# Two result rows in one PSUM bank, copied out by halves of their columns

## The chip, the cores and the metric

The kernel runs on one core of a Trainium2 chip. The metric is the device time of one execution in microseconds. The kernel before took 80.83 us (median of 3 runs, 80.6 to 80.95).

## The reference

One token `x` of 512 numbers goes through two branches whose results are mixed by a gate. Only the last 4096 positions of the caches of 65,536 are used.

```python
def _A_ref(x, k_cache, v_cache, wq, wo):      # 32 heads of queries, 8 of keys and values, 128 each
    W = min(4096, max(256, Sk // 4))          # 4096
    q = (x @ wq) as (heads, 1, 128)
    k, v = the last W positions of the caches, each repeated for 4 query heads
    p = _softmax((q · k) * 128 ** -0.5)
    return (p · v as 4096 numbers) @ wo       # 512

def _B_ref(x, w_gate, w_up, w_down):          # 512 -> 1792 -> 512
    return (_sigmoid(x @ w_gate) * (x @ w_up)) @ w_down

g = _sigmoid((x * gate_w).sum(-1, keepdims=True))
return g * _A_ref(...) + (1 - g) * _B_ref(...)
```

All inputs and the output are bf16. The output is one row of 512.

## The kernel before, in words

About 30 MB are read: `wq`, four pairs of K heads (`kn`), the gate and up weights, `wo`, four pairs of V heads (`vv`) and `w_down`, nearly all on the sync engine's DMA queue in the order of their use. The order of TensorE, VectorE and ScalarE is that of the text (`manual_schedule`, L187); only semaphore waits stand between them, and the framework puts those in from the tiles that an instruction reads and writes.

The queries are made first (L210 to L226), then the scores: each half pair of K is transposed by VectorE (L198) and multiplied into the score banks `S_ps` (L237). Softmax is by a maximum (L253 to L268), an exponential on ScalarE (L275) and a transpose to `eT` (L277). The gate and up projections (`glu`, L247) are put between these steps; each writes the partition groups 0, 32, 64 and 96 of one PSUM bank. For each pair of V heads, 16 matmuls (L316) sum into `pv_ps`. `pv_copy` (ScalarE, L322) moves two pairs' sums to SBUF, `heads_out` (L327 to L329) brings them into heads and divides by the softmax sum, and `heads_rows` (L334 to L336) leaves them as columns of `oY`.

The last step is the one that the change touches. `add_row` (L301 to L304) multiplies one column of 128 numbers by 512 columns of `wo` or `w_down`. It does it as two matmuls of 256 columns, one whose result is on partition 0 and one whose result is on partition 32, so that they use different column groups of the TensorE array. Both results accumulate in the PSUM tile `a_ps`, which spans two banks: the left half of the output row is in the first bank, the right half in the second. `out_rows` calls it for 32 columns of `oY` (64 matmuls) and the loop at L359 for 14 columns of `hT` (28 matmuls). In L358 and L359 the last 60 of these 92 follow one another.

Then the two halves are brought out (L362 to L366). VectorE copies row 0, 256 columns, to SBUF, and the sync queue stores it; ScalarE copies row 32, 256 columns, and its own queue stores it. Each store is one piece of 512 B.

Of the kernel before, what the change touches and what calls it, by code (L numbers as in the profile page):

```python
# [12 lines left out]
BF16 = mybir.dt.bfloat16  # L13
F32 = mybir.dt.float32
# [3 lines left out]
def kernel(  # L18
# [14 lines left out]
    nc = tc.nc  # L33

    P = 128
# [12 lines left out]
    N_OUT = A_wo.shape[1]  # L48
# [19 lines left out]
    work = ctx.enter_context(tc.tile_pool(name="work", bufs=1))  # L68
    ps_big = ctx.enter_context(tc.tile_pool(name="ps_big", bufs=2, space=bass.MemoryType.PSUM))
    ps_S = ctx.enter_context(tc.tile_pool(name="ps_S", bufs=2, space=bass.MemoryType.PSUM))  # L70
# [37 lines left out]
    wo_sb = big.tile([P, 2, NC_H, N_OUT], BF16, name="wo_sb", tag="big")  # L108
# [82 lines left out]
    for u in range(4):  # L191
        nc.tensor.matmul(S_ps[u // 2][:, u % 2, :], lhsT=other[:].rearrange("p o y u -> p (o y u)"),  # L192
                         rhs=ident[0:2, 0:2].rearrange("p (o y) -> p o y", o=1).to_broadcast([2, 256, 2]),
# [12 lines left out]
    for k in range(8):  # L206
        q_ps = ps_big.tile([P, 512], F32, name="q_ps", tag="b")
        ks = slice(k * 512, (k + 1) * 512)
        for c in range(DC):
            nc.tensor.matmul(q_ps[:], lhsT=xT[:, c:c + 1].to_broadcast([P, P]),  # L210
                             rhs=wq_sb[:, c, ks], start=(c == 0), stop=(c == DC - 1))
# [18 lines left out]
    for a in range(HP):  # L230
        for v in range(2):
            kT = kTs[a, v] if (a, v) in kTs else k_transpose(a, v)
            k_v = kT[:].rearrange("p (n dhi s t) -> p n dhi s t", n=KB, dhi=2, s=32)
            for dhi in range(2):
                for t in range(2):
                    for hb in range(2):
                        nc.tensor.matmul(S_ps[v][:, hb, :], lhsT=q_st[:, a, dhi, :, t],  # L237
                                         rhs=k_v[:, hb * 16:(hb + 1) * 16, dhi, :, t],
# [57 lines left out]

    HN = N_OUT // 2
    pv_ps = ps_S.tile([P, 2, 4 * P], F32, name="pv_ps", tag="S")
    a_ps = ps_S.tile([P, 2, 512], F32, name="a_ps", tag="S")

    def add_row(lhsT, rhs, start, stop):  # L301
        for i in range(2):
            nc.tensor.matmul(a_ps[32 * i:32 * i + 1, i, 0:HN], lhsT=lhsT, rhs=rhs[:, i * HN:(i + 1) * HN],  # L303
                             start=start, stop=stop)  # L304


# [5 lines left out]
    oY = work.tile([P, 2, NC_H], BF16, name="oY")  # L312
# [24 lines left out]

    def out_rows(hf, c0, c1):
        for c in range(c0, c1):
            add_row(oY[:, hf, c:c + 1], wo_sb[:, hf, c, :], hf == 0 and c == 0, False)  # L340

    pv(0)

# [8 lines left out]
    pv(3)  # L352
    pv_copy(1)
    out_rows(0, 0, NC_H // 2)
    heads_out(1)
    out_rows(0, NC_H // 2, NC_H)
    heads_rows(1)
    out_rows(1, 0, NC_H)  # L358
    for j in range(NJ):  # L359
        add_row(hT[:, j, 0:1], wd_sb[:, j, :], False, j == NJ - 1)  # L360

    res = work.tile([P, HN], BF16, name="res")  # L362
    nc.vector.tensor_copy(res[0:1, :], a_ps[0:1, 0, 0:HN])  # L363
    nc.sync.dma_start(out[0, :, 0:HN], res[0:1, :])
    nc.scalar.copy(res[32:33, :], a_ps[32:33, 1, 0:HN])
    nc.scalar.dma_start(out[0, :, HN:N_OUT], res[32:33, :])  # L366


# [28 lines left out]
```

## Time and profile before

| what | value |
|---|---|
| time, median of 3 | 80.83 us |
| span of the profiled execution | 80.0 us |
| TensorE busy | 56.9 us (71%) |
| VectorE busy | 39.2 us (49%) |
| ScalarE busy | 11.4 us (14%) |
| bytes read | 30.67 MB, 383 GB/s over the span |
| mean granted TensorE clock | 0.936 |
| last matmul issued to `a_ps` | 77.1 us, 272 ns long |

In the profile, L12 is line 12 of the kernel's source; DVE is VectorE, ACT is ScalarE, PE is TensorE, PEld its loads of the stationary operand, SPq and ACTq the sequencers of the sync engine and of ScalarE, which issue DMAs. A row of the timeline has the start, the length, the engine, the line, the operation, what is written and read, the shapes, and in brackets how long the engine had been idle and what released it. The chain of waits is followed back from the last instruction, at each step to what released it.

### The profile page before, as it was taken

To read this page: it belongs to the slowest core of one execution; us is meant where nothing else is said; L and a number is where in the kernel's file an instruction comes from. 1 tells how busy PE (TensorE), PEld (TensorE's weight loads), DVE (VectorE), ACT (ScalarE), POOL (GpSimd) and SP (SyncE) were. 2 spreads that over 40 slices of the span, in tenths; PEclk is the share of its full clock that TensorE was granted. 3 is DMA by queue.
4 is the path that set the end of the run, shared out by engine and by line. 5 is a ranking of instruction groups with operands and counts; after the bars stand their busy time and mean duration, and the time that the engine had idled before them with its cause. 6 is when DMAs were issued, how large, how long until landed. Compare 5 with 4: busy or idle time off the path is not lost.

```text
span 80.0 us, 833 instructions
## 1 busy us (share of the span) xinstructions
PE 56.9 (71%) x329; PEld 25.8 (32%) x329; DVE 39.2 (49%) x51; ACT 11.4 (14%) x21; POOL 3.7 (5%) x13
## 2 busy tenths in 40 slices
PE   0200194999941999988889365999698099998960
PEld 0200131333410334433333122444245033366840
DVE  0600820039449999999995519999500100002020
ACT  2400000225653000000000283000200000020010
POOL 7910000000000000000000000000000000000000
PEclk9999999999999579999999999999999755599999
DMA  6789989999999999999999999999999999998400
GB/s 181 262 344 525 426 360 393 434 451 426 410 459 434 410 451 414 444 392 425 407 449 467 401 401 451 459 393 410 451 430 385 430 459 451 381 393 344 152 0 1
DMA packets 2682, 30.71 MB, mean 384 GB/s; under 512 B 308, under 2 KB 440, under 8 KB 760
## 3 DMA queue, kind: packets, MB, share of 16 engines
q1 hardware_dynamic: 2674, 30.67, 91.3%
q8 instruction: 2, 0.03, 0.2%
q10 hardware_dynamic: 6, 0.00, 0.0%
HBM read 30.67 MB, written 0.00 MB: 383 GB/s over the span
## 4 chain that ended last, share of the span: by engine, by line
DMA 60%; PE 16%; DVE 14%; issue 4%; SPq 2%; DVEq 0%
DMA kn<-in_A_k_cache_dram 31%; DMA vv<-in_A_v_cache_dram 29%; DVE kT L198 13%; PE pv_ps L316 8%; PE a_ps L303 7%; SPq L85 2%; PE o_ps L327 1%; SPq L81 1%; DVE res L363 1%; DVE oY L336 0%; PE oY_ps L334 0%; DVEq L198 0%
## 5 line engine op out<-in xcount | busy, mean ns | idle before, releaser
L316 PE MATMUL pv_ps<-vv,eT 128*32 128x512 bf16 x64 | 17.4, 432 | 4.0 <-DMA vv<-in_A_v_cache_dram 1.7
L237 PE MATMUL S_ps<-kT,qbig 128*128 128x512 bf16 x64 | 16.3, 407 | 3.9 <-DVE qbig L226 2.8
L198 DVE STREAM_TRANSPOSE kT<-kn 128x2048 f32<-128x2048 f32 x8 | 17.8, 2278 | 0.0
L316 PEld LDWEIGHTS <-eT 128*32 128x32 bf16 x64 | 6.7, 107 | 13.7 <-issue 5.8
L237 PEld LDWEIGHTS <-qbig 128*128 128x128 bf16 x64 | 6.5, 102 | 13.7 <-issue 4.5
L210 PE MATMUL q_ps<-wq_sb,xT 128*128 128x512 bf16 x32 | 9.9, 484 | 1.2 <-DMA wq_sb<-in_A_wq_dram 1.2
L328 DVE TENSOR_TENSOR oT<-o_ps,rb 128x16 bf16<-128x16 f32 x2 | 0.3, 175 | 14.6 <-PE o_ps L327 14.6
L215 DVE STREAM_TRANSPOSE qtT<-q_sb 128x512 f32<-128x512 f32 x4 | 2.8, 712 | 8.0 <-ACT q_sb L212 8.0
L210 PEld LDWEIGHTS <-xT 128*128 128x128 bf16 x32 | 3.8, 118 | 7.8 <-issue 5.9
L192 PE MATMUL S_ps<-ident,other 2*128 2x512 bf16 x4 | 2.0, 611 | 5.7 <-DVE other L147 5.7
L212 ACT CAST q_sb<-q_ps 128x512 bf16<-128x512 f32 x8 | 4.7, 585 | 8.2 <-PE q_ps L210 8.2
L303 PE MATMUL a_ps<-wo_sb,oY 128*1 128x256 bf16 x64 | 5.2, 275 | 0.3 <-DVE oY L336 0.3
L322 ACT COPY pv_sb<-pv_ps 64x512 f32<-64x512 f32 x2 | 1.2, 578 | 21.4 <-PE pv_ps L316 21.4
L277 DVE STREAM_TRANSPOSE eT<-e_sb 128x1024 bf16<-128x1024 bf16 x2 | 2.4, 1224 | 1.9 <-ACT e_sb L275 1.9
L258 ACT ACTIVATE sge<-gu_ps 128x448 f32<-128x448 f32 x1 | 0.5, 543 | 18.9 <-PE gu_ps L247 18.9
L303 PEld LDWEIGHTS <-oY 128*1 128x1 bf16 x64 | 2.8, 83 | 1.2 <-DVE oY L336 0.4
L287 DVE RECIPROCAL sg<-sge 128x448 f32<-128x448 f32 x1 | 3.0, 2953 | 0.0
L175 DVE TENSOR_TENSOR gpr<-xr 1x512 f32<-1x512 bf16 x1 | 0.7, 680 | 4.6 <-DMA xr<-in_gate_w_dram 4.6
L253 DVE TENSOR_REDUCE pm<-S_ps 128x1 f32<-128x1024 f32 x2 | 2.4, 1204 | 0.9 <-PE S_ps L237 0.9
L155 PE MATMUL xt_ps<-ident,xr 1*128 1x1 bf16 x4 | 0.3, 164 | 3.5 <-POOL ident L131 3.5
L192 PEld LDWEIGHTS <-other 2*128 2x128 bf16 x4 | 0.6, 158 | 6.0 <-DVE other L147 5.8
L163 DVE COPY xp<-xr 1x64 bf16<-1x64 bf16 x2 | 1.2, 1162 | 2.0 <-DMA xr<-in_A_x_dram 2.0
(65 smaller groups left out, 33.5 us busy)
## 6 DMA issues: line engine op xcount, KB each, us to landing
kn<-in_A_k_cache_dram SPq DMA_DIRECT2D x4, 2048.0 KB, 20.9
vv<-in_A_v_cache_dram SPq DMA_DIRECT2D x3, 2048.0 KB, 19.4
wq_sb<-in_A_wq_dram SPq DMA_DIRECT2D x1, 4096.0 KB
wo_sb<-in_A_wo_dram SPq DMA_DIRECT2D x2, 2048.0 KB
vv<-in_A_v_cache_dram SPq DMA_DIRECT2D x2, 1024.0 KB
wg_sb<-in_B_w_gate_dram SPq DMA_DIRECT2D x1, 1792.0 KB
wu_sb<-in_B_w_up_dram SPq DMA_DIRECT2D x1, 1344.0 KB
wd_sb<-in_B_w_down_dram SPq DMA_DIRECT2D x1, 1024.0 KB
```

What stands on the lines that cost most here:

```text
L85: dq.dma_start(t[:, n0:n1, :].rearrange("p n d -> p (n d)"), cache[0, 2 * a:2 * a + 2, SBASE:SBASE + W, :] .rearrange("y (x n) d -> x y n ...
L192: nc.tensor.matmul(S_ps[u // 2][:, u % 2, :], lhsT=other[:].rearrange("p o y u -> p (o y u)"), rhs=ident[0:2, 0:2].rearrange("p (o y) -> p ...
L198: nc.vector.transpose(t[:].bitcast(F32), kn[a][:, v * KB:(v + 1) * KB, :] .rearrange("p n d -> p (n d)").bitcast(F32))
L210: nc.tensor.matmul(q_ps[:], lhsT=xT[:, c:c + 1].to_broadcast([P, P]), rhs=wq_sb[:, c, ks], start=(c == 0), stop=(c == DC - 1))
L212: nc.scalar.copy(q_sb[:, ks], q_ps[:])
L215: nc.vector.transpose(qtT[:].bitcast(F32)[:, kq], q_sb[:].bitcast(F32)[:, kq])
L237: nc.tensor.matmul(S_ps[v][:, hb, :], lhsT=q_st[:, a, dhi, :, t], rhs=k_v[:, hb * 16:(hb + 1) * 16, dhi, :, t], start=False, stop=(a == HP ...
L253: nc.vector.tensor_reduce(pm2[:, v:v + 1], S_ps[v][:].rearrange("p a b -> p (a b)"), axis=AX.X, op=ALU.max)
L277: nc.vector.transpose(eT[:, :, v * KB:(v + 1) * KB, :].rearrange("p a n r -> p n a r"), e_sb[:, v, :].rearrange("p (n a r) -> p n a r", a= ...
L287: nc.vector.reciprocal(sg[:], sge[:])
L303: nc.tensor.matmul(a_ps[32 * i:32 * i + 1, i, 0:HN], lhsT=lhsT, rhs=rhs[:, i * HN:(i + 1) * HN], start=start, stop=stop)
L316: nc.tensor.matmul(pv_ps[32 * (a % 2):32 * (a % 2) + 32, a // 2, :], lhsT=eT[:, a, 4 * m:4 * m + 4, :].rearrange("p n r -> p (n r)"), rhs= ...
```

## The change

Both halves of the output row are put in one PSUM bank. `a_ps` has 256 columns; the left half stays on partition 0 and the right half on partition 32. The copies are cut the other way: VectorE takes columns 0 to 127 of both rows, ScalarE columns 128 to 255 of both. A copy covers partitions 0 to 32 at once, 33 of them, of which two are wanted. So that the 31 partitions between hold written data, the very first pair of matmuls gets its column of `oY` repeated 32 times, which writes 32 partitions; all later ones write one. Each store then takes two pieces of 128 numbers (256 B), from partitions 0 and 32. The purpose is that each copy has half as many columns.

```diff
-    a_ps = ps_S.tile([P, 2, 512], F32, name="a_ps", tag="S")
+    a_ps = ps_S.tile([P, HN], F32, name="a_ps", tag="S")
 
     def add_row(lhsT, rhs, start, stop):
         for i in range(2):
-            nc.tensor.matmul(a_ps[32 * i:32 * i + 1, i, 0:HN], lhsT=lhsT, rhs=rhs[:, i * HN:(i + 1) * HN],
+            nc.tensor.matmul(a_ps[32 * i:32 * i + lhsT.shape[1], :], lhsT=lhsT, rhs=rhs[:, i * HN:(i + 1) * HN],
                              start=start, stop=stop)
...
     def out_rows(hf, c0, c1):
         for c in range(c0, c1):
-            add_row(oY[:, hf, c:c + 1], wo_sb[:, hf, c, :], hf == 0 and c == 0, False)
+            first = hf == 0 and c == 0
+            y = oY[:, hf, c:c + 1]
+            add_row(y.to_broadcast([P, 32]) if first else y, wo_sb[:, hf, c, :], first, False)
...
-    res = work.tile([P, HN], BF16, name="res")
-    nc.vector.tensor_copy(res[0:1, :], a_ps[0:1, 0, 0:HN])
-    nc.sync.dma_start(out[0, :, 0:HN], res[0:1, :])
-    nc.scalar.copy(res[32:33, :], a_ps[32:33, 1, 0:HN])
-    nc.scalar.dma_start(out[0, :, HN:N_OUT], res[32:33, :])
+    res = work.tile([33, HN], BF16, name="res")
+    out_v = out.rearrange("a b (i n) -> (a b i) n", i=2)
+    HH = HN // 2
+    nc.vector.tensor_copy(res[:, 0:HH], a_ps[0:33, 0:HH])
+    nc.sync.dma_start(out_v[:, 0:HH], res[0:33:32, 0:HH])
+    nc.scalar.copy(res[:, HH:HN], a_ps[0:33, HH:HN])
+    nc.scalar.dma_start(out_v[:, HH:HN], res[0:33:32, HH:HN])
```

## The prediction

> **What bounds the kernel now.** I read the page's chain of waits first, because the edit touches only the end of the program and the question is whether that end is on the chain. It is, for a small part. By line (fourth part of the page):
>
> ```profile
> DMA 60%; PE 16%; DVE 14%; issue 4%; SPq 2%; DVEq 0%
> DMA kn<-in_A_k_cache_dram 31%; DMA vv<-in_A_v_cache_dram 29%; DVE kT L198 13%; PE pv_ps L316 8%; PE a_ps L303 7%; SPq L85 2%; PE o_ps L327 1%; SPq L81 1%; DVE res L363 1%; DVE oY L336 0%; PE oY_ps L334 0%; DVEq L198 0%
> ```
>
> The loads of the K and V caches carry 60% of the chain. The edit adds and removes no load, so this part stays. What the edit can reach is "PE a_ps L303" (the output rows' matmuls) and "DVE res L363" (the copy out of PSUM). The same chain in order of time gives the last pieces, as start, length, what:
>
> ```profile
> 70.55 0.98 PE a_ps L303 x12
> 71.53 0.99 PE o_ps L327 x8
> 72.52 0.97 PE a_ps L303 x16
> ...
> 73.67 0.18 DVE oY L336
> 73.85 0.04 issue
> 73.90 3.48 PE a_ps L303 x60
> 77.38 0.40 DVE res L363
> ```
>
> So the last 60 matmuls run without a gap from 73.90 us, and the copy follows at once. The timeline of the last four microseconds shows what the chain leaves out, the second copy and the two issues:
>
> ```profile
> 77.37 0.41 DVE L363 CAST res<-a_ps 1x256 bf16<-1x256 f32 x1 [3.53 <-PE a_ps L303]
> 77.40 0.36 ACT L365 CAST res<-a_ps 1x256 bf16<-1x256 f32 x1 [6.13 <-PE a_ps L303]
> 77.80 0.23 ACTq L366 DMA_DIRECT2D out_dram<-res  x1
> 77.81 0.28 SPq L364 DMA_DIRECT2D out_dram<-res  x1
> ```
>
> Both copies are released by the matmuls and run side by side, one row each, one PSUM bank each. Both stores are issued within 0.01 us of each other. From there to the end of the span at 80.0 us are 2.2 us in which no engine computes: the stores land and the program closes. The edit doesn't touch that except by when and in what pieces the stores are issued.
>
> **What the Trainium skill says.**
> (1) "PSUM — Partial Sum Buffer", section "PSUM bank collisions raise a hardware error": two engines must not access the same bank in the same 32-partition quadrant at once, two reads included; other quadrants of a bank are fine. The trace of before neither confirms nor refutes it: its two copies read different banks and overlap by 0.36 us.
> (2) The same section says that different column tiles of TensorE may write one bank at the same time on disjoint partitions. The trace agrees, see below.
> (3) "DMA: Bandwidth & Descriptors", section "Specifications": below 512 B a transfer does a read-modify-write. Before stores 512 B a piece, so its trace can't show it.
> (4) The price of a copy is taken from the trace. "VectorE: DVE Perf Modes", section "The TRN2 errata", gives for a copy from PSUM a fixed part plus one cycle per element on either engine: (120 + n)/0.96 ns on VectorE and (172 + n)/1.2 ns on ScalarE, 392 and 357 ns for 256 columns as an estimate. The rows above have 413 and 362 by the groups' means, so the form holds.
>
> **The change, part by part.**
>
> *Both rows in one bank.* Row 0 stays on partition 0 and row 1 on partition 32, so each pair of matmuls still goes to two column groups of the array. Is a pair slowed when both write one bank? First, the present rate: 60 matmuls are 30 pairs in 3.44 us (73.90 to 77.34 by the timeline's 32 and 28), of which one matmul's tail belongs to no pair. The tail and the full pace come from the V matmuls: 16 of 512 columns, 379 ns each, take 3.63 us in a row (timeline at 48.93), so (3.63 - 0.38)/15 = 0.217 us from one to the next, 2.36 columns per ns, and a tail of 0.16 us. That leaves 3.28 / 30 = 109 ns a pair, and 256 columns at 2.36 per ns are 108. That is one stream's time for two matmuls; the pair runs together already. Second, the trace has a same-bank case, the gate projections at L247, which write four partition groups of one bank. The windows view of that line reads
>
> ```profile
> 43.00:44.10 1.10, 0.94 (x16) 0.33 (x16) 1.00 1.08 462
> ```
>
> with busy PE 0.94 us for 16 matmuls of 448 columns. Four rounds of 448 columns at 2.36 per ns are 0.76 us, plus the same tail of 0.16 makes 0.92. So four column groups write one bank with at most some 0.02 us lost over the whole group. I take 0 for the same-bank pair, upper bound 20 to 30 ns per 16 matmuls, up to 0.2 us over the 92 if the small remainder were all conflict.
>
> *The first pair has 32 columns of weights in place of one.* It fills 32 partitions so that the copy of 33 partitions reads only written data. The stationary loads of 128x32 take 97 ns against 84 for 128x1 (medians of L316 and L303), twice, at 69.2 us, under the last V matmuls that run until 70.55. The streamed columns are the same 256. Cost 0, hidden by the V matmuls.
>
> *The VectorE copy is 33x128 in place of 1x256.* Partitions work side by side, columns don't. From two PSUM copies on VectorE in this trace, 413 ns for 256 columns (L363) and 174 ns for 16 (L336), the slope is 239/240 = 1.0 ns a column; 128 columns take 174 + 112 = 286 ns. It ends at 77.37 + 0.29 = 77.66 and the sync queue's store is issued at about 77.69 in place of 77.81. A gain of 0.12 us on that half.
>
> *The ScalarE copy is 33x128 as well, and gets a wait.* In the compiled order of instructions before, it waits for TensorE alone, as the VectorE copy does. After, it waits for VectorE's semaphore. The two copies read the same bank in the same quadrant, and the framework puts one behind the other. So the point of halving, that both engines work at once, is gone: the copies form a chain. Behind the waiting copy on ScalarE stands only its own store, and the end of the program waits for that store. ScalarE's copy: 362 ns for 256 columns (L365) and 578 for 512 (L322) give 0.84 ns a column, so 128 take 362 - 108 = 254 ns. The hand-over from VectorE to ScalarE: in this trace a ScalarE copy of the queries starts 0.09 us after the VectorE transpose that it waits for ends (24.32 to 24.41 us), and VectorE to TensorE takes about 0.05 (73.85 to 73.90). I take 0.06, bounds 0.04 and 0.09. So ScalarE starts at 77.66 + 0.06 = 77.72, ends at 77.97, and its store is issued 0.04 later (as 77.76 to 77.80 before) at 78.01. Before, the later issue began at 77.81. That is +0.20 us at the start of the issue. The ScalarE issue took 0.23 us against 0.28 on the sync queue, so at its end it is 78.24 against 78.09, +0.15. I take +0.17.
>
> *Stores of two pieces.* Each store has two pieces of 256 B, on partitions 0 and 32, where it had one of 512 B; four pieces in all, the same 1 KB. Lower bound of the cost: 0, since they run beside each other. Upper bound: no row of before has such a store. If the read-modify-write of point 3 cost a read from HBM before the write, I allow 0.4 us, a fifth of the 2.2 us that the tail takes as a whole (an estimate from that length, no measurement). I take 0.02.
>
> The sum: -0 (matmuls) + 0.17 (chain of copies) + 0.02 (pieces) = +0.19 us, or 0.23%. 80.83 + 0.19 = 81.02, so I say 81.0.
>
> **The rivals.**
>
> *The intended gain arrives (chance 0.15).* The two half copies shorten the end because the sync queue's store, which comes to its end last now (78.09 against 78.03), is what closes the program, and the ScalarE store hides behind its longer landing. For it: only the VectorE copy is on the chain shown. Against: the ScalarE issue slips by 0.2 us and there is 0.06 us of slack between the two issues' ends. Time: 80.83 - 0.12 = 80.7; still no change by the bound. In the same case I count a truly parallel run, which would give the same.
>
> *The small stores cost (chance 0.20), the case on the slower side.* The chain of copies as above, plus read-modify-write or two completions to gather, at 0.3 to 0.4 us. For it: the skill's 512 B line and that the end waits for both stores. Against: 1 KB is nothing in bytes, and the store's landing is mostly fixed time. Time: 80.83 + 0.17 + 0.35 = 81.35, slower by 0.6%.
>
> *TensorE is slowed by the shared bank (chance 0.05).* At the upper bound, 0.2 us over 92 matmuls, of which the last 60 are on the chain for certain: +0.13 to +0.2 on top, 81.2. The gate projections speak against it.
>
> *Something in the loads shifts (chance 0.05).* 60% of the chain are loads, and three runs of before spread over 0.35 us. A faster stream might give 80.4 or less. Nothing in the edit drives it.
>
> **How the numbers follow.** The likeliest case, the copies in a chain with small stores at next to nothing, has 0.55 and gives 81.0. The low end takes in the intended gain with half the spread of the runs, 80.6; the high end takes in the costly stores, 81.4. About one time in five should fall outside. Faster by more than 0.5% means below 80.43: only the shifting loads and a small part of the intended gain, 0.07. Slower by more than 0.5% means above 81.23: most of the costly stores, and the tail of the others, 0.23. The rest, 0.70, is within.
>
> **What would show each step.** In the changed kernel's timeline: the VectorE copy of 33x128 near 0.29 us; the ScalarE copy of 33x128 near 0.25 us, starting only after the VectorE copy ends, with VectorE named as its releaser in place of TensorE; the two issues 0.3 us apart, the ScalarE queue's last; 60 matmuls of a_ps again in 3.44 us; and from the last issue to the end of the span about 2.0 us (78.01 to 80.0 or a little more). The chain's last piece would be the ScalarE copy. I am wrong if the two copies overlap, if the stretch after the last issue grows past 2.2 us (the stores' pieces), or if it shrinks by the whole slip so that the end doesn't move (the sync queue's store, or something else, closes the program).

## The result, and the profile after

The changed kernel takes 81.31 us (median of 6 runs) where the kernel before takes 80.84: a ratio of 1.006, 95% interval 1.0042 to 1.0077. It is slower by about 0.5 us. Some executions, whichever the kernel, take about 1.4 us longer; every ratio leaves these slow runs out, and where a profile is of one (starred in the table below), only its tail is read.

The profiled executions reach the end of the last matmuls about a microsecond apart (77.37 us before, 76.42 now), for reasons that lie ahead of the edit, so the two spans (80.0 and 79.7 us) say nothing here. What can be compared is the tail, from the start of the VectorE copy to the end of the span. In the trace it was 77.37 to 80.01 before, 2.64 us, and is 76.42 to 79.65 now, 3.23 us. It grew by 0.59 us, a little more than the loss of about 0.5 us that the times show.

The chain of waits of the changed kernel ends like this (start, length, what):

```profile
72.92 3.48 PE a_ps L303 x60
76.40 0.02 issue
76.42 0.29 DVE res L368
76.71 0.02 issue
76.74 0.26 ACT res L370
```

The 60 matmuls take the 3.48 us that they took before. One copy has become two in a row. The timeline of the same stretch adds the stores:

```profile
76.42 0.28 DVE L368 CAST res<-a_ps 33x128 bf16<-33x128 f32 x1 [3.56 <-PE a_ps L303]
76.73 0.59 SPq L369 DMA_DIRECT2D out_dram<-res  x1
76.74 0.26 ACT L370 CAST res<-a_ps 33x128 bf16<-33x128 f32 x1 [6.45 <-DVE res L368]
77.03 0.57 ACTq L371 DMA_DIRECT2D out_dram<-res  x1
```

Two things are to be seen. The ScalarE copy is released by VectorE and starts 0.04 us after that copy ends: they don't overlap at all. And each store takes 0.57 to 0.59 us to issue, where it took 0.23 and 0.28. The end of the program waits for the stores, and the sync engine's waits show it: before and after,

```profile
SPq L392 <- DMA out_dram<-res: 0.6, 1, 0.6
```

```profile
SPq L397 <- DMA out_dram<-res: 1.1, 2, 0.8
```

with the waited microseconds in total, the times and the longest. The issue of ScalarE's store began 0.43 us after the tail's start before (77.80) and begins 0.61 us after it now: 0.18 us, which I put down to the chain. From that issue to the end of the span there were 2.21 us (77.80 to 80.01) and there are 2.62 now: 0.41 us, which I put down to the stores. The two make 0.59. It is a division along one timeline; whether each part would be lost alone is for the experiments.

### The profile page after: what moved, and what is told of

It reads as the page before. It is cut to its first block, busy times and chain, and to the rows that moved or that the text cites. A ratio compares the mean times of both kernels' runs of the same rounds, so it can differ in the third digit from the quotient of the medians.

```text
span 79.7 us, 833 instructions
## 1 busy us (share of the span) xinstructions
PE 56.8 (71%) x329; PEld 25.8 (32%) x329; DVE 39.0 (49%) x51; ACT 11.3 (14%) x21; POOL 3.7 (5%) x13
## 4 chain that ended last, share of the span: by engine, by line
DMA 45%; PE 27%; DVE 16%; issue 7%; ACT 1%; DVEq 0%
DMA vv<-in_A_v_cache_dram 30%; DMA wq_sb<-in_A_wq_dram 15%; DVE kT L198 13%; PE q_ps L210 12%; PE a_ps L303 7%; PE pv_ps L316 7%; DVE qbig L226 2%; PE o_ps L327 1%; DVE qtT L215 1%; ACT q_sb L212 1%; DVE res L368 0%; ACT res L370 0%; DVE oY L336 0%; PE oY_ps L334 0%; DVEq L198 0%
## 5 line engine op out<-in xcount | busy, mean ns | idle before, releaser
L316 PE MATMUL pv_ps<-vv,eT 128*32 128x512 bf16 x64 | 17.9, 440 | 3.0 <-DVE eT L277 1.6
L210 PE MATMUL q_ps<-wq_sb,xT 128*128 128x512 bf16 x32 | 9.3, 462 | 1.4 <-DMA wq_sb<-in_A_wq_dram 1.4
L303 PE MATMUL a_ps<-wo_sb,oY 128*1 128x256 bf16 (+1 forms) x64 | 5.0, 274 | 0.3 <-DVE oY L336 0.3
L303 PEld LDWEIGHTS <-oY 128*1 128x1 bf16 (+1 forms) x64 | 2.9, 83 | 1.2 <-DVE oY L336 0.4
```

Source lines behind the costliest of these rows:

```text
L303: nc.tensor.matmul(a_ps[32 * i:32 * i + lhsT.shape[1], :], lhsT=lhsT, rhs=rhs[:, i * HN:(i + 1) * HN], start=start, stop=stop)
L316: nc.tensor.matmul(pv_ps[32 * (a % 2):32 * (a % 2) + 32, a // 2, :], lhsT=eT[:, a, 4 * m:4 * m + 4, :].rearrange("p n r -> p (n r)"), rhs= ...
```

## The experiments

After the result my theory was that the pieces of the stores cost most, some 0.4 us, and the chain of copies 0.17. Rival 1 was that the chain costs it all, rival 2 that the shared bank slows TensorE. The table has all twelve runs; each is told below. The tail is the one defined above, of one profiled execution each; the ratio is to the kernel before. The diffs are cut down to the lines that matter; the definitions of `res`, `out_v` and `HH` are left out where they are those of the changed kernel.

| run | copies | stores | tail, us | ratio (95% interval) |
|---|---|---|---|---|
| before | side by side | 2 of one piece | 2.64 | 1 |
| after | chain | 2 of two pieces | 3.23 | 1.0060 (1.0042 to 1.0077) |
| e1 | side by side | 2 of two pieces | 3.27 | 1.0089 (1.0072 to 1.0107) |
| e2 * | chain, whole rows | 2 of one piece | 2.88 | 1.0037 (1.0021 to 1.0053) |
| e3 | chain | 2 of one piece | 2.82 | 1.0030 (1.0017 to 1.0044) |
| e4 | one copy | 2 of one piece | 2.66 | 0.9997 (0.9984 to 1.0009) |
| f1 | side by side | 2 of two pieces, one queue | 3.62 | 1.0117 (1.0097 to 1.0136) |
| f2 | side by side | 4 of one piece, 256 B | 3.16 | 1.0081 (1.0063 to 1.0098) |
| f3 | side by side | 1 of two pieces, 512 B | 3.13 | 1.0058 (1.0044 to 1.0073) |
| f4 * | side by side | as e1, one queue warmed | 3.42 | 1.0124 (1.0073 to 1.0175) |
| g1 | side by side | 2 of two pieces, one partition | 3.25 | 1.0075 (1.0056 to 1.0095) |
| g2 | side by side | 2 of sixteen pieces | 3.38 | 1.0084 (1.0069 to 1.0099) |
| g3 * | side by side | 1 of one piece, ScalarE's queue | 2.60 | 0.9989 (0.9981 to 0.9996) |
| g4 | side by side | 1 of one piece, sync queue | 2.62 | 1.0000 (0.9988 to 1.0011) |

**e1, the stores alone.** The kernel before with the changed kernel's stores:

```diff
 nc.vector.tensor_copy(res[0:1, :], a_ps[0:1, 0, 0:HN])
-nc.sync.dma_start(out[0, :, 0:HN], res[0:1, :])
 nc.scalar.copy(res[32:33, :], a_ps[32:33, 1, 0:HN])
-nc.scalar.dma_start(out[0, :, HN:N_OUT], res[32:33, :])
+nc.sync.dma_start(out_v[:, 0:HH], res[0:33:32, 0:HH])
+nc.scalar.dma_start(out_v[:, HH:HN], res[0:33:32, HH:HN])
```

> Two banks and one row per engine as before, so the copies run side by side; only the stores are the changed kernel's, columns 0 to 127 of both rows and columns 128 to 255 of both, two pieces of 256 B each, and each store waits for both copies. My theory now (the stores' two pieces cost most of the loss, about 0.4 us of the 0.5): issues of about 0.57 us each in place of 0.28 and 0.23, time about +0.4 us against before, ratio 1.005. Rival 1 (the chain of the two copies costs it all): issues may be long, but the time is that of before, 1.000. Rival 2 (the shared bank slows TensorE): 1.000 too.

Its timeline:

```profile
76.25 0.41 DVE L365 CAST res<-a_ps 1x256 bf16<-1x256 f32 x1 [3.59 <-PE a_ps L303]
76.28 0.36 ACT L366 CAST res<-a_ps 1x256 bf16<-1x256 f32 x1 [6.20 <-PE a_ps L303]
76.72 0.59 SPq L367 DMA_DIRECT2D out_dram<-res  x1
76.73 0.57 ACTq L368 DMA_DIRECT2D out_dram<-res  x1
```

The copies are side by side, both released by TensorE, and the loss is there all the same: 1.0089, about 0.7 us. It is more than I expected (0.4), and no less than the changed kernel loses with its chain. Both rivals, at 1.000, fall.

**e2, a longer chain with stores of one piece.** One bank, but each engine copies a whole row and stores it:

```diff
+nc.vector.tensor_copy(res[0:1, :], a_ps[0:1, 0:HN])
+nc.sync.dma_start(out[0, :, 0:HN], res[0:1, :])
+nc.scalar.copy(res[32:33, :], a_ps[32:33, 0:HN])
+nc.scalar.dma_start(out[0, :, HN:N_OUT], res[32:33, :])
```

> The changed kernel's one bank and its first pair of 32 columns of weights, but each engine copies one whole row of 256 columns and stores it in one piece of 512 B. ScalarE waits for VectorE, so the chain is longer than in the changed kernel: 0.41 + 0.03 + 0.36 us, where the two ran side by side before. My theory (a chain costs what it delays the last issue by, and one-piece stores cost nothing): ScalarE's issue about 0.40 us later than before, time +0.35 to 0.40 us, ratio about 1.0045, issues of 0.2 to 0.3 us. Rival 1 (the chain costs it all): the changed kernel's last issue was 0.18 us later for 0.5 us lost, so here over +0.9 us, 1.011. Rival 2 (shared bank slows TensorE): the last 60 matmuls longer than 3.48 us.

```profile
77.81 0.41 DVE L366 CAST res<-a_ps 1x256 bf16<-1x256 f32 x1 [4.60 <-PE a_ps L303]
78.25 0.27 SPq L367 DMA_DIRECT2D out_dram<-res  x1
78.26 0.36 ACT L368 CAST res<-a_ps 1x256 bf16<-1x256 f32 x1 [7.61 <-DVE res L366]
78.65 0.23 ACTq L369 DMA_DIRECT2D out_dram<-res  x1
```

The chain is there although the rows lie in different quadrants of the bank: the framework keeps the engines apart by bank. The time is +0.30 us, a little under my 0.35 to 0.40 and far from rival 1's 0.9. The issue of ScalarE's store slipped by 0.41 us (from 0.43 to 0.84 after the tail's start) but the tail grew by only 0.24: the trace's packet records show why. Before, the sync queue's packet was the later one, 0.10 us after that of ScalarE's queue (78.62 against 78.51), so the first 0.1 us of the slip was slack. The rest lies in the landings. By the trace's semaphore records, which show when a store had landed, the sync queue's store, landing close behind the other, had landed 1.23 us after its issue began; in e2 ScalarE's store lands alone, in 1.08.

**e3, the changed kernel's chain alone.** Its copies of 33x128, but stores by rows:

```diff
-nc.sync.dma_start(out_v[:, 0:HH], res[0:33:32, 0:HH])
-nc.scalar.dma_start(out_v[:, HH:HN], res[0:33:32, HH:HN])
+nc.sync.dma_start(out[0, :, 0:HN], res[0:1, :])
+nc.scalar.dma_start(out[0, :, HN:N_OUT], res[32:33, :])
```

> The changed kernel with its one bank and its copies of 33x128, one behind the other, but each store takes one whole row, one piece of 512 B, and waits for both copies. My theory: only the chain is left, the issues about 0.17 us later than before and of 0.2 to 0.3 us, time +0.17 us, ratio 1.002. Rival 1 (chain alone): the full loss, 1.006. Rival 2 (shared bank): the full loss, 1.006.

```profile
76.43 0.28 DVE L367 CAST res<-a_ps 33x128 bf16<-33x128 f32 x1 [4.60 <-PE a_ps L303]
76.75 0.26 ACT L368 CAST res<-a_ps 33x128 bf16<-33x128 f32 x1 [7.49 <-DVE res L367]
77.03 0.27 SPq L369 DMA_DIRECT2D out_dram<-res  x1
77.03 0.23 ACTq L370 DMA_DIRECT2D out_dram<-res  x1
```

The chain is kept, the issues are short again, and half of the loss is gone: 1.003, +0.24 us, and +0.18 us of tail, which is the chain's price, with stores of one piece, as expected (0.17).

**e4, the bank alone.** One VectorE copy of both rows, no ScalarE copy, stores by rows:

```diff
-nc.vector.tensor_copy(res[:, 0:HH], a_ps[0:33, 0:HH])
-nc.scalar.copy(res[:, HH:HN], a_ps[0:33, HH:HN])
+nc.vector.tensor_copy(res[:], a_ps[0:33, :])
```

> The changed kernel's one bank, one VectorE copy of 33x256 for both rows, no ScalarE copy, each store one row of 512 B in one piece. No chain and no small pieces, only the shared bank is left. My theory: copy of 0.41 us, time as before, 1.000 within 0.001. Rival 1 (chain): 1.000. Rival 2 (the shared bank slows TensorE): 1.006, and the last 60 matmuls over 3.48 us.

```profile
76.53 0.42 DVE L366 CAST res<-a_ps 33x256 bf16<-33x256 f32 x1 [4.59 <-PE a_ps L303]
76.97 0.28 SPq L367 DMA_DIRECT2D out_dram<-res  x1
76.98 0.23 ACTq L368 DMA_DIRECT2D out_dram<-res  x1
```

The ratio is 0.9997 (0.9984 to 1.0009). The shared bank and the first pair with 32 columns of weights cost nothing that can be measured, and 33 partitions are copied in the time of one. In this trace the last 60 matmuls do stretch over more than 3.48 us, because the last 28 wait twice for the load of `w_down` (idle for 0.37 and 0.17 us); the runs f1 and f3 with two banks have the same waits, and the 22 and 6 matmuls that follow them take 1.43 and 0.61 us here, 1.44 and 0.60 there.

So the store of two pieces is the larger part. What about it? Four runs on the kernel before, with only its last lines changed (and in f4 a store at the start). The theories: the form (more than one piece), the size (256 B), or the first use of the form on a queue.

**f1, both two-piece stores on one queue.** Against e1:

```diff
 nc.sync.dma_start(out_v[:, 0:HH], res[0:33:32, 0:HH])
-nc.scalar.dma_start(out_v[:, HH:HN], res[0:33:32, HH:HN])
+nc.sync.dma_start(out_v[:, HH:HN], res[0:33:32, HH:HN])
```

> Copies as before (two banks, side by side). Both stores of two 256 B pieces are issued by the sync queue, one after the other, none by ScalarE. Is the long issue a property of the form, or of the first use of that form on a queue? Theory form (two pieces on two partitions always take long to issue): both issues 0.55 to 0.6 us, the time about 0.6 us above the run with one such store on each queue, ratio to before about 1.016. Theory first use: first issue 0.59, second about 0.28 us, ratio about 1.012. Theory size (256 B pieces are what costs): silent on the issues.

```profile
76.84 0.59 SPq L367 DMA_DIRECT2D out_dram<-res  x1
77.47 0.53 SPq L368 DMA_DIRECT2D out_dram<-res  x1
```

The second issue is nearly as long as the first, as the theory of form says. The time, 1.0117 (1.0097 to 1.0136), agrees with the 1.012 that I had given to first use and not with the 1.016 of form, a miss. For 1.016 I had added the second issue in full to the time of e1. The last issue does begin 0.62 us later than in e1 (1.11 against 0.49 us after the tail's start), but its store, which now lands alone, has landed after 1.52 us in place of 1.74. So what speaks for form here is the length of the issue, not the time.

**f4, one queue warmed.** e1, and ScalarE also issues a store of the same form at the start:

```diff
+    zero = const.tile([33, N_OUT // 4], BF16, name="zero")
+    nc.gpsimd.memset(zero[:], 0.0)
+    nc.scalar.dma_start(out.rearrange("a b (i n) -> (a b i) n", i=2)[:, N_OUT // 4:N_OUT // 2], zero[0:33:32, :])
```

> Copies as before and one two-piece store of 256 B pieces on each queue at the end, as in the first of these runs, but ScalarE also issues a store of the same form at the start of the program (zeros, overwritten at the end), so its queue has used the form once and the sync queue has not. Theory first use: ScalarE's early issue 0.5 us or more, its last issue about 0.25 us; the sync queue's still 0.59. Theory form: ScalarE's last issue 0.57 us again. Time in both near that of the run without the early store, 1.007 to 1.009, because the sync queue's store is unchanged.

```profile
3.94 0.55 ACTq L148 DMA_DIRECT2D out_dram<-zero  x1
...
78.29 0.59 SPq L372 DMA_DIRECT2D out_dram<-res  x1
78.30 0.50 ACTq L373 DMA_DIRECT2D out_dram<-res  x1
```

The warmed queue saves 0.07 us of 0.57. First use is not the cause. The time doesn't tell the theories apart, which gave the same range. The mean, 1.0124, lies above that range, but three of its five runs took 81.39 us, 1.008 of the kernel before and within it; the other two, at 82.04 and 82.45, make the interval wide.

**f2, four stores of one piece of 256 B.**

```diff
+nc.sync.dma_start(out_v[0:1, 0:HH], res[0:1, 0:HH])
+nc.scalar.dma_start(out_v[1:2, 0:HH], res[32:33, 0:HH])
+nc.sync.dma_start(out_v[0:1, HH:HN], res[0:1, HH:HN])
+nc.scalar.dma_start(out_v[1:2, HH:HN], res[32:33, HH:HN])
```

> Copies as before. Four stores of one piece of 256 B each, two on each queue, so the pieces have the size of the changed kernel's but each has its own issue. Theory form: each issue 0.23 to 0.28 us, the last begins about 0.3 us later than before, time +0.3 us, ratio 1.0035. Theory size (pieces under 512 B land slowly): the issues may be short but the end comes 0.5 us or more later, ratio 1.006 or above. Theory first use: as theory form.

```profile
76.86 0.23 ACTq L368 DMA_DIRECT2D out_dram<-res  x1
76.87 0.28 SPq L367 DMA_DIRECT2D out_dram<-res  x1
77.13 0.26 ACTq L370 DMA_DIRECT2D out_dram<-res  x1
77.20 0.29 SPq L369 DMA_DIRECT2D out_dram<-res  x1
```

The issues are short, 0.23 to 0.29 us, at the same 256 B: the size doesn't make an issue long. But the time, 1.0081 or +0.65 us, is a miss: form alone had +0.3 us, and size had 1.006 or above. So is it the size after all? The semaphore records say no. The first two stores had landed 1.06 and 1.23 us after their issues began, at 256 B; before, at 512 B, it was 1.07 and 1.23. The tail's +0.52 us splits so: the last issue begins 0.77 us after the tail's start, before 0.44 (+0.33); its store has landed 1.25 us later, before 1.23 (+0.02); and from there to the end of the span are 1.14 us, before 0.97 (+0.17). The last part is the sync engine's: it goes through its final waits one by one, about 0.06 us each. Before, the store that lands last is the last waited for; in f2 it is the first that holds the engine up (0.9 us), and three more waits follow it.

**f3, one store of both rows, pieces of 512 B.**

```diff
+nc.sync.dma_start(out_v, res[0:33:32, :])
```

> Copies as before. One store in all, on the sync queue: both rows, two pieces of 512 B each from partitions 0 and 32. Theory form: issue of 0.55 to 0.6 us, the time +0.5 us, ratio 1.006. Theory size (256 B is what costs): issue 0.28 us and the time of before, 1.000. Theory first use: as theory form.

```profile
76.91 0.59 SPq L367 DMA_DIRECT2D out_dram<-res  x1
```

Two pieces of 512 B take as long to issue as two of 256 B, and the ratio is 1.0058. By the packet records its first packet comes 1.23 us after the start of the issue, where the one piece of before on the same queue took 0.81: +0.42 us of the tail's +0.49. Of the 0.42 the issue itself is 0.31 (0.59 against 0.28); the rest passes between its end and the first packet. The theory of size, which gave 1.000, falls.

**g1 and g2, pieces from one partition.** Is it the two partitions or the two pieces? Each engine copies its own row, but leaves a gap of 16 numbers after 128 columns (g1) or after every 16 (g2), so a store takes 2 pieces of 256 B or 16 of 32 B from one partition:

```diff
+res = work.tile([33, 2, 144], BF16, name="res")          # g2: [33, 16, 32]
+nc.vector.tensor_copy(res[0:1, :, 0:128], ...)
+nc.sync.dma_start(out_v[0:1], res[0:1, :, 0:128])        # ScalarE the same with row 32
```

> Copies as before, each engine its own row, but each copy leaves a gap of 16 numbers after 128 columns, so each store takes two pieces of 256 B from one partition and each waits for its own copy alone, as before. What in the form makes the issue long? Theory pieces (any two pieces): issues 0.55 to 0.6 us, time +0.55 us, ratio 1.007. Theory partitions (two partitions as the source): issues 0.23 to 0.28 us, ratio 1.000 to 1.001.

> As the run with two pieces from one partition, but a gap after every 16 columns: each store has 16 pieces of 32 B from one partition. The loads of w_down, 128 pieces each, were issued in 0.33 us, less than the 0.57 of two pieces. Theory uneven split (a count that fills only part of the 16 engines costs the long issue): 16 pieces are issued in about 0.33 us, time +0.1 to +0.2 us, ratio 1.002. Theory pieces (more than one piece is long, with the loads short for another reason): 0.57 us or more, ratio 1.007 or above.

The issues of g1 and then of g2:

```profile
76.72 0.68 ACTq L367 DMA_DIRECT2D out_dram<-res  x1
76.73 0.68 SPq L365 DMA_DIRECT2D out_dram<-res  x1
```

```profile
76.82 0.58 ACTq L367 DMA_DIRECT2D out_dram<-res  x1
76.83 0.61 SPq L365 DMA_DIRECT2D out_dram<-res  x1
```

One partition doesn't help: 0.68 us. Sixteen pieces take no longer than two. So what costs is that a store has more than one piece, hardly how many, how large, or on how many partitions. What makes such an issue long was not found. Why the loads of `w_down`, 128 pieces each, are issued in 0.33 us (three of the four at L125), where the other loads of the sync queue took from 0.41 to 0.82, is open too; the uneven split that I had offered fell with g2.

**g3 and g4, one piece in all.** If having more than one piece costs, and each store has to be waited for, the best store is one of 1 KB from one partition. The copies may put both rows there:

```diff
-    res = work.tile([P, HN], BF16, name="res")
+    res = work.tile([1, N_OUT], BF16, name="res")
-    nc.vector.tensor_copy(res[0:1, :], a_ps[0:1, 0, 0:HN])
-    nc.sync.dma_start(out[0, :, 0:HN], res[0:1, :])
-    nc.scalar.copy(res[32:33, :], a_ps[32:33, 1, 0:HN])
-    nc.scalar.dma_start(out[0, :, HN:N_OUT], res[32:33, :])
+    nc.vector.tensor_copy(res[:, 0:HN], a_ps[0:1, 0, 0:HN])
+    nc.scalar.copy(res[:, HN:N_OUT], a_ps[32:33, 1, 0:HN])
+    nc.scalar.dma_start(out[0, :, :], res[:])             # g4: nc.sync
```

> A version meant to beat both kernels: two banks and side-by-side copies as before, but both land on one partition of one tile, and ScalarE's queue issues one store of 1 KB in one piece after both. My theory: a one-piece store costs the same whatever its length here, and ScalarE's store went out 0.05 us quicker than the sync queue's (0.23 against 0.28), and the end waits for one store and not two: time -0.1 us, ratio 0.998 to 1.000. If the length or a copy to another partition costs something: 1.001 or above.

> The same with the store on the sync queue. My theory: the sync queue's store was the later one of before, so this is the time of before or a little less, ratio 0.999 to 1.001, about 0.1 us above the one on ScalarE's queue.

```profile
77.89 0.41 DVE L363 CAST res<-a_ps 1x256 bf16<-1x256 f32 x1 [4.62 <-PE a_ps L303]
77.92 0.36 ACT L364 CAST res<-a_ps 1x256 bf16<-1x256 f32 x1 [7.22 <-PE a_ps L303]
78.37 0.23 ACTq L365 DMA_DIRECT2D out_dram<-res  x1
```

On ScalarE's queue the ratio is 0.9989 (0.9981 to 0.9996), about 0.1 us below the kernel before; on the sync queue 1.0000 (0.9988 to 1.0011). A copy to another partition costs nothing: 0.41 and 0.36 us as before. The version with one store on ScalarE's queue beats both kernels, by little: 0.03 to 0.15 us by the interval, and 0.04 us by the tail.

## Why the prediction was right or wrong

The range held the time (81.31 between 80.6 and 81.4), but the case that I called likeliest, no change at 81.0, did not come. What came is the time of the rival that had 0.20, "The small stores cost", at 81.35, and for a reason other than the one given there. That the number fell within the range is in part luck.

*The matmuls.* Right. The last 60 take 3.48 us on both chains, and e4 shows the shared bank at 0.9997. The gate projections in the trace of before had pointed to it. The Trainium skill's sentence on column tiles in one bank ("PSUM — Partial Sum Buffer", "PSUM bank collisions raise a hardware error") agrees.

*The first pair.* Right: it starts under the V matmuls, and e4 contains it at no cost.

*The copies' lengths.* Right: 286 ns forecast and 0.28 us measured on VectorE, 254 ns and 0.26 us on ScalarE, hand-over 0.06 and 0.04.

*The chain of copies.* Right in kind, and in size where the stores have one piece. ScalarE is released by VectorE, the later issue comes 0.17 us later against the tail's start (0.61 against 0.44; 0.20 forecast), and e3 alone shows 0.18 us of tail and +0.24 us of time (1.0030, interval 1.0017 to 1.0044) for the 0.17 taken. It does not add to the cost of the long stores: e1, which has them without the chain, is no faster than the changed kernel (1.0089 against 1.0060).

*Stores of two pieces.* This is the step that failed: "I take 0.02". It measured 0.41 us in the changed kernel, and alone, in e1, 0.63 us of tail. The step priced the pieces only by what their bytes and their landing might cost, and passed over the issue: it carried 0.23 and 0.28 us over from the rows of before, which were issues of one piece. On ScalarE's queue, whose store ends the program, the issue took 0.57 us in place of 0.23, and from its end to the first packet it took 0.73 us in place of 0.49. The upper bound of 0.4 us, given for the read-modify-write that the Trainium skill has below 512 B ("DMA: Bandwidth & Descriptors", "Specifications"), had about the right size but the wrong mechanism. On the sync queue a store of two pieces of 512 B (f3) had landed 1.60 us after its issue began, one of two pieces of 256 B in the changed kernel 1.59; and a single piece of 256 B (f2) is issued and lands as fast as one of 512 B. Whether these stores do a read-modify-write no run shows; if they do, it cost nothing that the landings show. The trace of before could have warned: its issue rows run from 0.21 us, for the second load of one piece on ScalarE's queue, to over 0.5 us for others, the first such load among them, so an issue is no constant, and none of its rows was a small transfer of several pieces.

*The intended gain.* Wrong as I thought: half the columns took 0.13 us off VectorE's copy, and the wait put two halves one after the other.

*What doesn't add up, and why.* The chain alone (+0.18 us of tail) and the stores alone (+0.63) make 0.81, the changed kernel has 0.59. The semaphore records divide each tail by the store that lands last (in us, rounded):

| run | its issue begins | issue to landing | landing to the end | tail |
|---|---|---|---|---|
| before | 0.44, sync | 1.23 | 0.97 | 2.64 |
| after | 0.61, ScalarE | 1.66 | 0.97 | 3.23 |
| e1 | 0.49, ScalarE | 1.74 | 1.04 | 3.27 |
| e3 | 0.60, sync | 1.26 | 0.96 | 2.82 |

In the changed kernel the chain sets the two stores 0.3 us apart. ScalarE's starts 0.12 us later than in e1, but lands 0.08 us quicker, and it is the last that the sync engine waits for, where in e1 one more wait follows (0.07 us). So in these traces, with stores of two pieces, the chain gives back what it takes. Why a store that lands close to another takes longer was not tried.

## What to carry to other kernels

At the end of this kernel the output store's issue and landing are all on the path. Where that is so, give it one piece, and let the copies gather the row in one partition, rather than save columns of the copy. With this framework two engines shared the work of emptying PSUM only when they read different banks; in one bank they stood in line, also on different partitions (e2), so halving the columns gave two halves in a row. A duration taken over from a row of the profile holds for that form of the instruction; when an edit changes the form of a transfer, its issue is a cost to be bounded too.

## What the runs showed of the hardware that was not expected

A store with more than one piece took 0.50 to 0.68 us to issue where one of one piece took 0.23 to 0.29, be it 2 or 16 pieces, 32, 256 or 512 B, on one partition or two, and on the sync queue its first packet came 1.22 to 1.51 us after the start of the issue against 0.75 to 0.83. A single piece of 256 B landed as soon as one of 512 B (1.06 and 1.07 us after the start of the issue on ScalarE's queue, 1.23 and 1.23 on the sync queue). The sync engine's waits at the end of the program took about 0.06 us each, one after the other, so four stores had a longer end than two (1.14 against 0.97 us after the last landing). A copy of 33 partitions took the time of one (0.42 against 0.41 us for 256 columns), and one whose result goes from partition 32 to partition 0 took no longer (0.36 us on ScalarE).
